# A new step list for block 0, other mask order, 54-key strided scores and a split last store

## The chip, the cores and the metric

One core of a Trainium2 chip runs the whole program once. The metric is device time in microseconds (us) of that core, the median of several runs. The engines have in-order queues of their own: TensorE (PE, with PEld for its weight loads), VectorE (DVE), ScalarE (ACT), GpSimd (POOL), and SyncE (SP), which here only issues DMAs. ACT issues a few DMAs too, from its own queue, between its activations.

## The reference

Eight batches of eight heads attend over 576 tokens (head width 64): four heads look back over 32 tokens, four over the tokens of the same remainder modulo 32. The attention output, 4608 tokens by 512, then goes through a gated layer of width 2048.

```python
scores = scale * np.matmul(q, k.transpose(0, 1, 3, 2))
mask_local = (rel >= 0) & (rel < stride)
mask_strided = (rel >= 0) & (pos[None, :] % stride == pos[:, None] % stride)
scores = np.where(masks[None, :, :, :], scores, -1000000000.0)
scores = scores - np.max(scores, axis=-1, keepdims=True)
attn = np.exp(scores)
attn = attn / (np.sum(attn, axis=-1, keepdims=True) + 1e-09)
return np.matmul(attn, v).astype(np.float32)
...
h = x @ w_in
g = h * (1.0 / (1.0 + np.exp(-h)))
return (g @ w_out).astype(np.float32)
```

## The kernel before

The layer runs in nine blocks of 512 tokens. A block has 16 chunks of 128 hidden columns; a chunk is 12 products of 128x512 for the hidden values (L623) and 12 for the output (L687), because each float32 operand is kept as a rounded high part and a low part and three of the four cross products are taken. Over the nine blocks this makes 3456 products, nearly all of PE's work.

Attention is cut into groups, six per batch: three local ones of 12 tiles of 32 queries, and three strided ones of 8, 8 and 6 tiles of 54 queries padded to 64. The first batch (groups 0 to 5) must be through before the first block can start, and in block 0 the weights are also split into their two parts. From block 1 on the groups of the next batches are worked between the chunks.

Everything up to the end of block 0 follows a list written out by hand, `PLAN` (L104): a word is a step, `~n` is n idle products of 128x128 on PE, and a letter behind a dot picks the engine. `follow` (L163) issues the steps in the order of the list, each on its own engine, and each engine works its steps in that order. For a group c: `k` and `v` load, `S` scores (PE, L402), `M` masking and row maximum (DVE, L422), `E` exponentials (ACT, L439, one per column of tiles and head), `R` reciprocal of the sum (DVE), `N` scaling (DVE or POOL, L458), `T` transposition (PE), `P` copy of it (DVE or ACT, L468), `O` product with v, `Q`, `X`, `B` the way back to x. `H0c` and `L0c` make the high and low part of x. For a piece i of weights: `p` load, `a` two activations (ACT, L266, L271), `j` (DVE, L277), `b` the high part (L318), `d` the low part (L322). For a chunk: `h` and `i` the two halves of the hidden products, `t`, `g`, `w`, `l` the gate and its two parts, `o` the output products. The first product, `h0`, needs `d0`, `L00` and `L01`.

Loads of k are split in block 0, and the second half of groups 0 to 2 is issued by ACT:

```python
ways = (load, nc.scalar.dma_start if a.at < 3 else load)
for some, way in zip(halved(n, 1 if a.b else 2), ways):
    way(out=kbds[kbd_of(a.b, a.at)][:, :, some], in_=kqt[a.b, a.gi, :, :, some])
```

POOL makes the masks at the start (L210 to L240): local ones of 64 keys, wide local ones of 96 keys (used from group 14 on), then the strided one, which group 3 is the first to use.

Of the kernel before, what the change touches and what calls it, by code (L numbers as in the profile page):

```python
# [13 lines left out]
F32 = mybir.dt.float32  # L14
# [10 lines left out]
DM, DFF = 512, 2048  # L25
STRIDE = 32
# [75 lines left out]
RATE = 310e3  # L102

PLAN = """  # L104
k0 k1 k2 k3 v0 ~9 S0 M0 k4 v1 E0 ~1 S1 k5 M1 E1 v2 ~1 S2 M2 E2 R0 ~2 T0 P0.D p0 S3 M3 E3 ~3 T1
P1.D R1 O0 Q0 S4 k6 M4 E4 v3 p1 T2 P2.D X0 B0.D O1 Q1 ~5 X1 R3 R2 S5 v4 B1.D v5 M5 E5 O2 N3.P
T3 p3 p5 H00.D R4 N4.P Q2 ~4 X2 P3.D L00.D R5 S6 B2.A H01.D N5.D a0 j0 L01.D T4 P4.A b0.D p2 a1
j1 d0.D O3 b1.D p4 k8 T5 P5.A O4 O5 d1.D p7 B3 p6 B4 H02.D L02.D B5 H03.A L03.D M6 a3 j3 b3.D
d3.D p9 a5 j5 a2 h0 h1 i0 t0 g0 i1 j2 t1 g1 h2 b5.A d5.D S8 k10 i2 w0.A l0.D h3 b2.A d2.D o0 v7
p11 a4 j4 b4.D d4.D w1.A l1.P M8 t2 g2 p8 a7 j7 b7.D S10 w2.D d7.D i3 p10 a9 j9 a6 j6 E8 R8  # L110
N8.D h4 b9.A o1 d9.P t3 g3 h5 M10 p13 E6 p15 v6 b6.D d6.D p12 k7 R6 l2.D o2 a10 j10 a11 j11
b11.D d11.D p17 h6 i4 a8 j8 i5 i6 a13 j13 b13.D w3.A l3.D N6.D V6 b8.A d8.P p14 o3 E10 t4 d13.P
p19 a15 j15 g4 O6 b10.A d10.P p16 t5 g5 h7 b15.D d15.D p21 a12 j12 v8 w4.A l4.D o4 a17 j17
b17.D d17.D p23 R10 i7 w5.A b12.A d12.D p18 a14 j14 a19 j19 B6 t6 g6 S7 k9 h8 l5.D o5 a16 j16
b16.D d16.D p22 V8 k12 M7 i8 t7 g7 O8 h9 v10 N10.P b19.A d19.P w6.A l6.P b14.A d14.D o6 p20 i9
a21 j21 a18 j18 b18.D a23 j23 b23.D w7.A l7.D o7 d23.D p25 a22 j22 b22.D d22.D p24 B8 E7 R7
N7.D t8 g8 h10 w8.A S9 l8.P k11 i10 V7 t9 g9 b21.A d21.P h11 d18.P o8 M9 a20 j20 a24 j24 b24.D
d24.D p26 t10 g10 h12 S11 k13 i12 b20.A d20.D i11 a25 j25 b25.D d25.D p27 E9 R9 V10 M11 w10.A
l10.P w9.A l9.P o9 t12 g12 t11 g11 N9.P a26 j26 b26.A d26.P p28 O7 B7 V9 v9 a27 j27 b27.D d27.D
O10 B10 E11 R11 N11.D o10 w11.A l11.P w12.A l12.P S12 M12 V11 a28 j28 b28.D d28.P E12 R12 N12.P  # L120
h13 h14 i13 t13 g13 i14 t14 g14 p29 a29 j29 b29.A d29.P O9 B9 v11 V12 o11 w13.A l13.P S13 M13
o12 w14.D l14.D p30 a30 j30 b30.D d30.D O11 B11 H10.A L10.D H11.A L11.D h15 H12.A H13.A L12.D
L13.D p31 a31 j31 b31.D d31.P o13 i15 t15 g15 w15.D l15.D E13 R13 N13.D V13 o14
"""


# [49 lines left out]
def sparse_attention_ffn(ctx: ExitStack, tc: tile.TileContext, kqt, vt, w_in, w_out, out):  # L176
# [31 lines left out]
    def mask(name, columns=72):  # L208
        m = const.tile([P, columns], F32, name=name)
        nc.gpsimd.memset(m, 0.0)  # L210
        return m
# [30 lines left out]
    nc.gpsimd.memset(ones, 0.0)
    for h in range(2):
# [43 lines left out]
    def halved(n, parts):  # L287
        return [slice(i * n // parts, (i + 1) * n // parts) for i in range(parts)]
# [62 lines left out]
    class Attention:  # L351


        def __init__(self, b, at):
            self.b, self.at, self.gi = b, at, order_of(b)[at]
            self.by_blocks = b * NG + at >= TURNED
            self.g = g = GROUPS[self.gi]
            self.spread = b * NG + at in SPREAD
            self.sums_by_pe = self.spread and g.local and not self.by_blocks
            self.kbd, self.vbd = kbds[kbd_of(b, at)], vbds[vbd_of(b, at)]  # L360
            self.cols = g.n * P
            self.wide = g.local and b * NG + at >= WIDE_FROM
# [15 lines left out]

        def halves(self, banks):

            n, keys = self.g.n, self.keys
            return [t[:, : n * keys].rearrange("p (c k) -> p c k", k=keys) for t in banks]

        def scores(self, banks=None):
            g, kbd = self.g, self.kbd
            self.pss = banks or [self.bank("pss") for _ in range(2)]
            if self.wide:
                for t in (0, 6, 2, 8, 4, 10):
                    c, r = self.at_of[t]
                    rows = slice(r * STRIDE, (r + 2) * STRIDE)  # L390
                    for h in range(2):
                        at = slice(h * D, (h + 1) * D)
                        nc.tensor.matmul(  # L393
                            self.pss[h][rows, c * WIDE : (c + 1) * WIDE],
                            kbd[at, 1, g.q0[t] : g.q0[t] + 2 * STRIDE],
                            kbd[at, 0, g.k0[t] : g.k0[t] + WIDE], start=True, stop=True,
                        )
                return
            for t, c, rows in self.tiles:
                for h in range(2):  # L400
                    at = slice(h * D, (h + 1) * D)
                    nc.tensor.matmul(  # L402
                        self.pss[h][rows, c * KW : (c + 1) * KW],
                        kbd[at, 1, g.q0[t] : g.q0[t] + g.rows],
                        kbd[at, 0, g.k0[t] : g.k0[t] + KW], start=True, stop=True,
                    )

        def peak(self):
            g = self.g
            s_ps = self.halves(self.pss)  # L410
            self.sm = att.tile([P, 640], F32, name="sm", bufs=3)
            self.s_sb = self.sm[:, : g.n * 2 * self.keys].rearrange(
                "p (c h k) -> p c h k", h=2, k=self.keys
            )
# [661 lines left out]
```

## Time and profile before

| | us |
|---|---|
| median of 3 runs (871.29 to 871.56) | 871.31 |
| the profiled execution | 871.88 |
| its span, first to last instruction | 870.1 |
| PE busy in the span | 862.5 |
| DVE, ACT, POOL busy | 514.1, 318.7, 40.3 |

The span is what the trace shows; 1.8 us of the profiled execution lie around it. A row of the timeline gives the start, the time to the end of the last one, engine, line, operation, tiles, shapes and how many equal ones were merged, and in brackets the idle time just before with the releaser. PE's ends are modelled and its products overlap, so starts are the better clock. In a table of stretches the columns are the stretch, its length, busy time and count of each engine, the granted PE clock as a share, the DMA engines' share and GB/s. A float32 product appears as two records.

### The profile page before, as it was taken

What the parts mean: (1) busy time and instruction counts of PE and PEld (TensorE: products, weight loads), DVE (VectorE), ACT (ScalarE), POOL (GpSimd) and SP (SyncE); (2) the same over time, 40 slices, a digit from 0 to 9 for tenths busy, and PEclk for the clock granted to TensorE, in tenths of its full rate; (3) what the DMA queues carried; (4) which work ended last, traced back from release to release, by engine and by line L of the source; (5) the groups of instructions that cost most, each with busy time, mean ns of one, the idle gap of its engine ahead of it and who ended that gap; (6) DMA issues with size and microseconds to landing.
All of it is one profiled execution on the core that took longest, in us unless ns stands there. A gap on an engine that the chain in (4) does not pass through costs nothing.

```text
span 870.1 us, 17241 instructions
## 1 busy us (share of the span) xinstructions
PE 862.5 (99%) x6809; PEld 707.9 (81%) x6809; DVE 514.1 (59%) x1602; ACT 318.7 (37%) x1070; POOL 40.3 (5%) x68
## 2 busy tenths in 40 slices
PE   8999999999999999999999999999999999999998
PEld 5777788888888888888888888888888888888886
DVE  6999887558556647656655855664762533343333
ACT  7987863315413333333431541333331311131111
POOL 5023320000000000000000000000000000000000
PEclk9999999999999999999999999999999999999999
DMA  9976443202302212220320230221210000000001
GB/s 293 288 251 221 142 157 95 72 2 76 118 1 72 77 50 68 72 77 18 100 73 1 77 117 1 72 76 50 69 29 1 29 20 1 1 27 22 1 1 49
DMA packets 37041, 64.55 MB, mean 74 GB/s; under 512 B 2912, under 2 KB 23776, under 8 KB 36960
## 3 DMA queue, kind: packets, MB, share of 16 engines
q1 hardware_dynamic: 36144, 62.79, 22.3%
q8 instruction: 53, 0.87, 0.4%
q10 hardware_dynamic: 816, 0.66, 0.2%
q14 instruction: 28, 0.23, 0.1%
HBM read 54.00 MB, written 9.44 MB: 73 GB/s over the span
## 4 chain that ended last, share of the span: by engine, by line
PE 92%; DVE 3%; ACT 2%; issue 1%; POOL 1%; POOLq 0%; DVEq 0%; ACTq 0%
PE po L687 44%; PE ps L623 43%; PE ps L526 3%; PE ps L393 1%; PE ps L402 1%; DVE stage L277 1%; DVE sm L422 1%; ACT stage L271 0%; ACT stage L266 0%; POOL mask_local L215 0%; DVE th L655 0%; DVE w L318 0%; ACT xb L566 0%; DVE w L322 0%; ACT sm L439 0%
## 5 line engine op out<-in xcount | busy, mean ns | idle before, releaser
L623 PE MATMUL ps<-xhi,w 128*128 128x512 f32 x1152 | 376.7, 390 | 0.5 <-DVE th L655 0.5
L623 PEld LDWEIGHTS ps<-xhi,w 128*128 128x128 f32 x1152 | 216.2, 188 | 46.0 <-DVE th L655 0.7
L655 DVE SCALAR_TENSOR_TENSOR th<-th,ps 128x512 f32<-128x512 f32 (+1 forms) x147 | 99.2, 675 | 258.6 <-ACT th L633 257.7
L633 ACT ACTIVATE th<-ps 128x512 f32<-128x512 f32 (+1 forms) x147 | 86.7, 590 | 448.3 <-PE ps L623 416.5
L623 PE MATMUL ps<-xlo,w 128*128 128x512 f32 x576 | 224.2, 389 | 0.0
L687 PE MATMUL po<-w,ghi 128*128 128x512 f32 x504 | 156.9, 392 | 0.0
L623 PEld LDWEIGHTS ps<-xlo,w 128*128 128x128 f32 x576 | 108.1, 188 | 22.2
L439 ACT ACTIVATE sm<-sm,sums 128x64 f32<-128x64 f32 (+1 forms) x320 | 109.2, 348 | 2.9 <-DVE sums L422 2.9
L687 PEld LDWEIGHTS po<-w,ghi 128*128 128x128 f32 x504 | 93.7, 188 | 20.0 <-DVE w L322 0.3
L667 DVE TENSOR_TENSOR glo<-th,ghi 128x512 fp32r<-128x512 f32 (+1 forms) x139 | 95.7, 689 | 11.9
L687 PE MATMUL po<-w,glo 128*128 128x512 f32 x252 | 98.4, 390 | 0.4 <-DVE glo L667 0.4
L687 PE MATMUL po<-stage,ghi 128*128 128x512 f32 x288 | 88.8, 389 | 0.0
L486 DVE STREAM_TRANSPOSE pt<-sm 32x192 f32<-32x192 f32 (+1 forms) x168 | 65.8, 392 | 3.0
L687 PE MATMUL po<-v,ghi 128*128 128x512 f32 x216 | 67.5, 394 | 0.0
L663 DVE CAST ghi<-th 128x512 fp32r<-128x512 f32 (+1 forms) x134 | 56.6, 422 | 12.8 <-PE po L687 1.2
L687 PEld LDWEIGHTS po<-stage,ghi 128*128 128x128 f32 x288 | 54.0, 188 | 11.2
L439 ACT ACTIVATION_READ_ACCUMULATOR sm<-sm,sums 128x1 f32 x320 | 61.8, 193 | 0.0
L687 PEld LDWEIGHTS po<-w,glo 128*128 128x128 f32 x252 | 47.3, 188 | 11.1 <-DVE glo L667 1.1
L687 PE MATMUL po<-stage,glo 128*128 128x512 f32 x144 | 56.0, 389 | 0.0
L687 PEld LDWEIGHTS po<-v,ghi 128*128 128x128 f32 x216 | 39.9, 188 | 8.4
L687 PE MATMUL po<-k,ghi 128*128 128x512 f32 x144 | 44.3, 389 | 0.0
L687 PE MATMUL po<-v,glo 128*128 128x512 f32 x108 | 42.0, 389 | 0.0
(77 smaller groups left out, 676.9 us busy)
## 6 DMA issues: line engine op xcount, KB each, us to landing
out<-stage SPq DMA_DIRECT2D x36, 256.0 KB, 2.0
v<-vt SPq DMA_DIRECT2D x21, 384.0 KB, 5.4
stage<-w_out SPq DMA_DIRECT2D x14, 512.0 KB, 4.3
k<-kqt SPq DMA_DIRECT2D x14, 512.0 KB, 4.9
stage<-w_in SPq DMA_DIRECT2D x12, 512.0 KB, 4.4
k<-kqt SPq DMA_DIRECT2D x14, 416.0 KB, 3.9
v<-vt SPq DMA_DIRECT2D x14, 256.0 KB, 5.4
k<-kqt SPq DMA_DIRECT2D x7, 448.0 KB, 3.9
```

The source lines that it names most:

```text
L277: nc.vector.scalar_tensor_tensor(out=upper, in0=upper, scalar=3, in1=lower, op0=ALU.logical_shift_left, op1=ALU.bitwise_or,)
L393: nc.tensor.matmul(self.pss[h][rows, c * WIDE : (c + 1) * WIDE], kbd[at, 1, g.q0[t] : g.q0[t] + 2 * STRIDE], kbd[at, 0, g.k0[t] : g.k0[t] ...
L402: nc.tensor.matmul(self.pss[h][rows, c * KW : (c + 1) * KW], kbd[at, 1, g.q0[t] : g.q0[t] + g.rows], kbd[at, 0, g.k0[t] : g.k0[t] + KW], s ...
L439: nc.scalar.activation(out=self.s_sb[:, c, h], in_=self.s_sb[:, c, h], func=AF.Exp, bias=self.peaks[:, c, h : h + 1], scale=-1.0, accum_ou ...
L486: nc.vector.transpose(out=pt[to, r % 2], in_=src[rows, 1 if self.wide else 1 - r % 2])
L526: nc.tensor.matmul(self.pso[p][h * D : (h + 1) * D, i * size : (i + 1) * size], vbd[at, 2 * i + h], moved, start=True, stop=True,)
L623: nc.tensor.matmul(ph, weight(0, wi, fc)[:, cc * P : (cc + 1) * P], x[xi][cc], start=(cc, n) == (0, 0), stop=(cc, n) == (NP - 1, 2),)
L633: nc.scalar.activation(out=th[:, cols], in_=ph[:, cols], func=AF.Tanh, scale=0.5)
L655: nc.vector.scalar_tensor_tensor(out=th[:, cols], in0=th[:, cols], scalar=1.0, in1=ph[:, cols], op0=ALU.add, op1=ALU.mult,)
L663: copy[engine](out=g[0][:, cols], in_=th[:, cols])
L667: either[engine].tensor_sub(out=g[1][:, cols], in0=th[:, cols], in1=g[0][:, cols].bitcast(F32))
L687: nc.tensor.matmul(po[tt], g[gi][:, cols], weight(1, wi, fc), start=fc == 0 and n == 0, stop=fc == NFC - 1 and n == 2,)
```

## The change

The list for block 0 is new. No subtraction `d` or `l` is on POOL until `d21`; in their place the two subtractions `L00` and `L01` are there. Steps change place throughout; the loads `k1`, `k2`, `k3` come behind `S0 M0 E0` and `S1`. The idle words sum to 21 instead of 25. POOL makes the wide masks behind the strided one. From group 14 on strided scores have 54 keys instead of 64, and POOL zeroes the ten columns left over in the tile `sm`. The very last store is cut into two halves, one scaled by DVE and stored by SP, one scaled and stored by ACT.

```diff
-k0 k1 k2 k3 v0 ~9 S0 M0 k4 v1 E0 ~1 S1 k5 M1 E1 v2 ~1 S2 M2 E2 R0 ~2 T0 P0.D p0 S3 M3 E3 ~3 T1
+k0 ~7 S0 M0 E0 k1 ~1 S1 k2 k3 v0 M1 E1 k4 R0 v1 ~3 S2 M2 E2 T0 P0.D R1 k5 v3 ~2 S3 M3 E3 T1
...
-    for wide, keys in ((False, KW), (True, WIDE)):
+    for wide, keys in ((False, KW),):
...
     masks[None, ()] = m
+    for wide, keys in ((True, WIDE),):
+        m = mask(f"mask_local{keys}", keys + 8)
...
+            self.seen = SEQ if not g.local and b * NG + at >= WIDE_FROM else self.keys
...
-                        self.pss[h][rows, c * KW : (c + 1) * KW],
+                        self.pss[h][rows, c * self.seen : (c + 1) * self.seen],
                         kbd[at, 1, g.q0[t] : g.q0[t] + g.rows],
-                        kbd[at, 0, g.k0[t] : g.k0[t] + KW], start=True, stop=True,
+                        kbd[at, 0, g.k0[t] : g.k0[t] + self.seen], start=True, stop=True,
...
+            if self.seen < self.keys:
+                pad = self.sm[:, : g.n * 2 * KW].rearrange("p (c k) -> p c k", k=KW)
+                nc.gpsimd.memset(pad[:, :, self.seen :], 0.0)
...
+            if (k, tt) == (NBLK - 1, NTT - 1):
+                r0 = k * T + tt * P
+                for some, engine in zip(halved(DM, 2), (nc.vector, nc.scalar)):
+                    if engine is nc.vector:
+                        nc.vector.tensor_scalar_mul(osb[:, some], po[tt][:, some], 0.5)
+                        nc.sync.dma_start(out=out[r0 : r0 + P, some], in_=osb[:, some])
+                    else:
+                        nc.scalar.mul(out=osb[:, some], in_=po[tt][:, some], mul=0.5)
+                        nc.scalar.dma_start(out=out[r0 : r0 + P, some], in_=osb[:, some])
+                continue
```

ACT at the start of the program, before: k_80 to k_82 are the tiles of groups 0 to 2, and an ACTIVATE at L439 (L457 in the changed file) is one of the exponentials `E`, six of them for a local group.

```order
L337 DMA k_80<-kqt 128x2x208
L337 DMA k_81<-kqt 128x2x224
L337 DMA k_82<-kqt 128x2x208
L439 ACT_TABLE_LOAD
L439 ACTIVATE sm,sums<-sm,sums 128x64 x40
L582 COPY xb<-po 128x3x4x32
```

ACT at the same place in the changed kernel:

```order
L351 DMA k_80<-kqt 128x2x208
L457 ACT_TABLE_LOAD
L457 ACTIVATE sm,sums<-sm,sums 128x64 x6
L351 DMA k_81<-kqt 128x2x224
L351 DMA k_82<-kqt 128x2x208
L457 ACTIVATE sm,sums<-sm,sums 128x64 x28
L617 CAST xhi<-xb 128x512
L457 ACTIVATE sm,sums<-sm,sums 128x64 x6
```

The second halves of k1 and k2 moved from ahead of all exponentials to behind the six of group 0, and `H00` moved in ahead of the last six.

POOL between the end of the masks and its third subtraction, before (xlo is the low part of x, glo of the gate, w of the weights, sm the scores):

```order
L242 MEMSET ones 128x2
L244 MEMSET ones 64x1 x2
L458 TENSOR_TENSOR sm<-sm,sums 128x512 x2
L667 TENSOR_TENSOR glo<-th,ghi 128x512
L322 TENSOR_TENSOR w_0_665<-stage_755,w_0_657 128x512
```

POOL at the same place in the changed kernel:

```order
L256 MEMSET ones 128x2
L258 MEMSET ones 64x1 x2
L476 TENSOR_TENSOR sm<-sm,sums 128x512
L621 TENSOR_TENSOR xlo<-xb,xhi 128x512 x2
L336 TENSOR_TENSOR w_0_696<-stage_1125,w_0_694 128x512
```

One scaling of scores left POOL, and the two low parts of x came to it, ahead of the first weights.

## Rows read from the trace of the kernel before

**Rows 1.** The page's first line, and three stretches from the table of stretches (columns as said above).

```profile
span 870.1 us, 17241 instructions
...
13.00:26.30 13.30, 12.06 (x315) 8.85 (x315) 12.89 (x60) 12.24 (x54) 2.09 (x2) 1.00 1.01 314
...
40.00:70.00 30.00, 29.11 (x234) 22.81 (x211) 29.36 (x64) 25.69 (x73) 7.67 (x6) 1.00 0.83 272
...
150.00:860.00 710.00, 710.00 (x5115) 588.51 (x5114) 381.45 (x1136) 203.10 (x701) 0.00 (x0) 1.00 0.14 45
```

**Rows 2.** Timeline of PE from its first idle products to `h0`: idle products, `S0`, `S1`, and the first product of `h0`.

```profile
1.37 4.21 PE L781 MATMUL ps<-ident 128*128 128x512 f32 x6 [1.37 <-POOL ident masks.py:199]
5.51 0.87 PE L402 MATMUL ps<-k 64*32 64x64 f32 x48
...
6.72 0.84 PE L402 MATMUL ps<-k 64*32 64x64 f32 x48
...
26.32 0.50 PE L623 MATMUL ps<-xhi,w 128*128 128x512 f32 x1
```

**Rows 3.** Timeline of ACT: its three DMA issues, the first exponential of `E0` and the first of `E1`.

```profile
0.74 2.23 ACTq L337 DMA_DIRECT2D k<-kqt  x3
...
6.86 0.35 ACT L439 ACTIVATE sm<-sm,sums 128x64 f32<-128x64 f32 x1 [2.58 <-DVE sums L422]
...
8.87 0.34 ACT L439 ACTIVATE sm<-sm,sums 128x64 f32<-128x64 f32 x1
```

**Rows 4.** DMA issues by line, with KB each and median us from issue to landing: the k loads issued by 1.0 us and by 2.5 us (ACT's), SP's loads of v issued from 7 to 11 us, and the stores of the whole run.

```profile
k<-kqt ACTq DMA_DIRECT2D x1, 208.0 KB, 4.0
...
k<-kqt ACTq DMA_DIRECT2D x1, 224.0 KB, 4.4
...
v<-vt SPq DMA_DIRECT2D x3, 192.0 KB, 4.3
...
out<-stage SPq DMA_DIRECT2D x36, 256.0 KB, 2.0
```

**Rows 5.** Timeline of DVE: the first instruction of `M0`, of `M1`, of `M3`, and `d0`.

```profile
6.59 0.23 DVE L422 CUSTOM_DVE_ANT_0 sm<-ps,mask 128x64 f32<-128x64 f32 x1 [6.59 <-PE ps L402]
...
7.71 0.23 DVE L422 CUSTOM_DVE_ANT_0 sm<-ps,mask 128x64 f32<-128x64 f32 x1 [0.17 <-POOL mask_local L215]
...
11.74 0.22 DVE L422 CUSTOM_DVE_ANT_0 sm<-ps,mask_strided 128x64 f32<-128x64 f32 x1 [1.08 <-POOL mask_strided L215]
...
24.89 0.69 DVE L322 TENSOR_TENSOR w<-stage,w 128x512 fp32r<-128x512 f32 x1
```

**Rows 6.** Groups of DVE instructions by form (busy us, mean ns of one, idle before them): `N` of a strided group of 8, `L`, `P` of 512 and of 384 columns; and from the timeline the start of `M6` and of the instruction behind it.

```profile
L458 DVE TENSOR_TENSOR sm<-sm,sums 128x512 f32<-128x512 f32 x13 | 9.0, 693 | 0.5
L603 DVE TENSOR_TENSOR xlo<-xb,xhi 128x512 fp32r<-128x512 f32 x8 | 5.5, 698 | 0.6 <-ACT xhi L599 0.6
L468 DVE COPY pt<-po 128x384 f32<-128x384 f32 x3 | 1.6, 541 | 0.0
L468 DVE COPY pt<-po 128x512 f32<-128x512 f32 x1 | 0.7, 679 | 0.0
28.61 0.22 DVE L422 CUSTOM_DVE_ANT_0 sm<-ps,mask 128x64 f32<-128x64 f32 x1
29.48 0.69 DVE L277 SCALAR_TENSOR_TENSOR stage<-stage 128x512 int32<-128x512 int32 x1
```

**Rows 7.** Timeline of POOL and DVE where they meet: a subtraction on POOL and the high part of a weight made by DVE inside it; the same DVE operation with POOL idle; another subtraction on POOL and DVE's transpositions inside it.

```profile
36.09 1.31 POOL L667 TENSOR_TENSOR glo<-th,ghi 128x512 fp32r<-128x512 f32 x1 [14.99 <-ACT ghi L663]
36.27 1.41 DVE L318 CAST w<-stage 128x512 fp32r<-128x512 f32 x1
...
30.20 0.43 DVE L318 CAST w<-stage 128x512 fp32r<-128x512 f32 x1
...
56.33 1.33 POOL L322 TENSOR_TENSOR w<-stage,w 128x512 fp32r<-128x512 f32 x1 [0.97 <-ACT w L318]
56.48 1.54 DVE L486 STREAM_TRANSPOSE pt<-sm 32x192 f32<-32x192 f32 x4
```

**Rows 8.** Timeline of PE in block 0: the rows before which it waited, each with the row ahead of it.

```profile
47.33 0.75 PE L687 MATMUL po<-w,ghi 128*128 128x512 f32 x2
48.46 0.50 PE L687 MATMUL po<-w,glo 128*128 128x512 f32 x1 [0.38 <-DVE glo L667]
...
66.15 0.69 PE L402 MATMUL ps<-k 64*64 64x64 f32 x32
67.36 0.50 PE L623 MATMUL ps<-xhi,w 128*128 128x512 f32 x1 [0.51 <-DVE th L655]
```

**Rows 9.** PE's strided scores in the timeline with the row behind them; and two groups by form, with 64 and with 54 columns moved.

```profile
83.77 0.69 PE L402 MATMUL ps<-k 64*64 64x64 f32 x32
84.39 0.50 PE L623 MATMUL ps<-xhi,w 128*128 128x512 f32 x1
...
L402 PE MATMUL ps<-k 64*64 64x64 f32 x704 | 15.5, 221 | 0.3 <-DVE sums L422 0.3
L526 PE MATMUL ps<-pt,v 64*64 64x54 f32 x616 | 13.2, 221 | 0.0
```

**Rows 10.** The end: one of the stretches in which the last four stores are written, and in the timeline ACT's scaling of the last output tile.

```profile
866.25:866.50 0.25, 0.07 (x1) 0.00 (x0) 0.18 (x1) 0.09 (x1) 0.00 (x0) 1.00 1.05 401
...
866.41 0.60 ACT L701 ACTIVATE stage<-po 128x512 f32<-128x512 f32 x1 [0.76 <-PE po L687]
```

More of the change, by code (lines that the diff above doesn't have):

```diff
@@ L104 @@
 PLAN = """
-k0 k1 k2 k3 v0 ~9 S0 M0 k4 v1 E0 ~1 S1 k5 M1 E1 v2 ~1 S2 M2 E2 R0 ~2 T0 P0.D p0 S3 M3 E3 ~3 T1
[L106 to L122, printed above, removed]
@@ L123 @@
-L13.D p31 a31 j31 b31.D d31.P o13 i15 t15 g15 w15.D l15.D E13 R13 N13.D V13 o14
+k0 ~7 S0 M0 E0 k1 ~1 S1 k2 k3 v0 M1 E1 k4 R0 v1 ~3 S2 M2 E2 T0 P0.D R1 k5 v3 ~2 S3 M3 E3 T1
+P1.D R2 v2 O0 Q0 p0 ~2 S4 k6 M4 X0 B0.D O1 Q1 R3 N3.P E4 T2 P2.D ~3 X1 B1.D H00.A S5 M5 O2 p1
+v4 T3 E5 R4 N4.D ~3 T4 v5 Q2 X2 B2.A p3 P3.D a0 P4.D L00.P R5 H01.D N5.D O3 B3 p5 p2 j0 L01.P
+S6 M6 k8 T5 P5.D a1 j1 b0.A d0 b1.D d1 p7 O4 B4 H02.A L02 p4 p6 O5 h0 h1 B5 H03.D L03 i0 i1 a3
+j3 b3.D a5 j5 d3 h2 p9 a2 j2 t0 g0 S8 k10 b5.A d5 p11 t1 g1 h3 w1.D b2.A d2 p8 i2 v6 w0.A l0 o0
@@ new lines @@
+l1 M8 i3 a7 j7 b7.D E6 R6 d7 p13 a4 j4 t2 g2 S10 k12 h4 N6 a9 j9 b4.A d4 o1 p10 a6 j6 M10 b9.A
+d9 p15 a11 j11 v7 i4 b6.A d6 p12 t3 g3 h5 V6 O6 v8 E8 R8 b11.A d11 p17 i5 a8 j8 N8 w2.A l2 o2
+a13 j13 a10 j10 b8.A d8 p14 t4 g4 h6 w3.A l3 o3 i6 b13.A d13 k7 a15 j15 b15.D d15 p21 b10.A d10
+p16 w4.A l4 o4 B6 t5 p19 a17 j17 b17.D d17 p23 g5 h7 S7 k9 i7 E10 R10 w5.D l5 a14 j14 t6 g6 h8
+a12 j12 b12.D d12 o5 p18 a21 j21 b21.D w6.A l6 a16 j16 i8 b14.A d14 p20 o6 a19 j19 a23 j23
+b16.A d16 p22 M7 V8 d21.P b23.A d23.P p25 t7 g7 w7.D l7 O8 v10 h9 o7 i9 b19.A d19 E7 R7 N7 a20
@@ new lines @@
+j20 B8 a22 j22 b22.D d22.D p24 t8 g8 h10 S9 i10 k11 a18 j18 a25 j25 b18.A d18 t9 g9 h11 M9 V7
+w8.A l8.P o8 b25.A d25.P p27 b20.A d20.P t10 g10 h12 S11 i12 a24 j24 b24.D d24.D p26 N10 V10
+M11 E9 w10.A l10.P i11 w9.A l9.P t12 o9 g12 t11 g11 O10 R9 N9 a27 j27 a26 j26 b26.D d26.D p28
+E11 R11 N11.P b27.A d27.P B10 O7 V9 B7 V11 v9 o10 w11.A l11.P w12.A l12.P S12 M12 a28 j28 b28.D
+d28.D E12 R12 N12.P h13 h14 i13 i14 t14 g14 t13 g13 O9 V12 B9 p29 a29 j29 b29.D d29.D o11 w13.A
+l13.P k13 S13 M13 p30 a30 j30 b30.D d30.D o12 w14.A l14.D v11 O11 B11 H10.A H11.A L11.D L10.D
@@ L124 @@
+h15 H12.A H13.A L13.D L12.D p31 a31 j31 b31.D d31.D o13 i15 t15 g15 w15.D l15.D E13 R13 N13.D
+V13 o14
 """
@@ L240, in sparse_attention_ffn @@
     masks[None, ()] = m
+    for wide, keys in ((True, WIDE),):
+        m = mask(f"mask_local{keys}", keys + 8)
+        for t in range(P // STRIDE):
+            ahead = STRIDE * (t % 2) if wide else 0
+            keep(m, t * STRIDE, STRIDE, [keys], [1], -1 - ahead, -1)
+            keep(m, t * STRIDE, STRIDE, [keys], [-1], STRIDE + ahead, 1)
+        masks[wide, ()] = m
+        some = {s for g in GROUPS for s in (g.paired_starts if wide else g.starts) if s}
+        for starts in sorted(some):
+            first = const.tile([P, keys + 8], F32, name=f"mask{keys}_" + "".join(map(str, starts)))
+            nc.gpsimd.tensor_copy(out=first, in_=m)
+            for t in starts:
+                keep(first, t * STRIDE, STRIDE, [keys], [1], -STRIDE, 0)
+            masks[wide, starts] = first
     ones = const.tile([P, 2], F32, name="ones")
@@ L379, in halves @@
         def halves(self, banks):
-            n, keys = self.g.n, self.keys
+            n, keys = self.g.n, self.seen
             return [t[:, : n * keys].rearrange("p (c k) -> p c k", k=keys) for t in banks]
@@ L413, in peak @@
                 "p (c h k) -> p c h k", h=2, k=self.keys
-            )
+            )[:, :, :, : self.seen]
+            if self.seen < self.keys:
+                pad = self.sm[:, : g.n * 2 * KW].rearrange("p (c k) -> p c k", k=KW)
+                nc.gpsimd.memset(pad[:, :, self.seen :], 0.0)
             s_sb = self.s_sb
@@ L417, in peak @@
             self.peaks, self.rsum = peaks, rsum = sums[:, 0, : g.n], sums[:, 1, : g.n]
-            self.inv = rsum.unsqueeze(3).broadcast_to([P, g.n, 2, self.keys])
+            self.inv = rsum.unsqueeze(3).broadcast_to([P, g.n, 2, self.seen])
             for c in range(g.n):
@@ L422, in peak @@
                     nc.vector.tensor_tensor_reduce(
-                        out=s_sb[:, c, h], in0=s_ps[h][:, c], in1=self.masks[c][:, : self.keys],
+                        out=s_sb[:, c, h], in0=s_ps[h][:, c], in1=self.masks[c][:, : self.seen],
                         scale=-SCALE, scalar=BIG, op0=ALU.add, op1=ALU.min,
@@ L428, in lessen @@
         def lessen(self):
-            peaks = self.peaks.unsqueeze(3).broadcast_to([P, self.g.n, 2, self.keys])
+            peaks = self.peaks.unsqueeze(3).broadcast_to([P, self.g.n, 2, self.seen])
             nc.gpsimd.tensor_sub(self.s_sb, self.s_sb, peaks)
```

## The prediction

> **What bounds the kernel now.** I read the table of stretches first, then the timelines of PE, ACT and DVE in the first 30 us, the DMA issues, and last the few waits of PE. From 150 to 860 us PE is busy throughout, and DVE, ACT and the DMA engines are far from full [rows 1]. Products start in a fixed pace there, so nothing that DVE or ACT do in the later blocks can show. What can change is the time before the first product `h0`, at 26.32 us [rows 2], the waits of PE in block 0, and the end. In the head ACT and DVE are nearly full (12.24 and 12.89 of 13.30 us), and in block 0 DVE is (29.36 of 30) [rows 1]. The chain of the head runs: k0 lands, `S0`, `M0`, `E0`, then the exponentials of all groups one after the other on ACT, with DVE between, until `d0` at 24.89 to 25.58 [rows 5]; PE comes to `h0` 0.74 later.
>
> **The loads on ACT's queue.** This is the term on which I rest. Before, ACT issues its three halves of k0, k1 and k2 from 0.74 on and then waits for `M0` [rows 3]. In the new order the halves of k1 and k2 stand behind the six exponentials of `E0` on the same in-order queue, and `E0` waits for `M0`, `S0` and k0. Behind them in turn wait `S1`, `M1`, `E1`, and SP, whose load of k5 writes the tile that `S1` reads.
>
> When do they go out? Nine idle units before `S0` take 5.51 - 1.37 = 4.14 us, 0.46 each [rows 2]; seven take 3.2, to 4.6. k0 was issued at 0.74 and takes 4.0 to land [rows 3, 4], so `S0` starts at 4.8 instead of 5.51, and `E0` at 6.15 instead of 6.86. Six exponentials take 8.87 - 6.86 = 2.01 [rows 3]; the issue comes at 8.1. For the landing the rows give 2.0 (a lone store, late in the run) up to 4.4 (the load of k1 itself, with the start's traffic) and 4.3 (v, 7 to 11 us) [rows 4]. SP has fewer loads in flight here than in those, since it stops at k5, but more than none: I take 3.2, so the half is there at 11.3. Two of the twelve tiles of `S1` need only the first half; the other ten and the step to DVE take about 0.9 of the 7.71 - 6.72 = 0.99 that `S1` to `M1` took [rows 2, 5]. `M1` starts at 12.2 instead of 7.71: +4.5 us. Bounds: 11.0 and 13.4.
>
> **From `M1` to `d0` on DVE.** Before, this took 25.58 - 7.71 = 17.87 us. The new list puts in ahead of `d0`: two copies `P` that were ACT's (0.68 and 0.54), `M6` (29.48 - 28.61 = 0.87) and one scaling `N` (0.69); it takes out `L00` and `L01` (0.70 each), a high part of a weight and one of x (0.43 each, by the weight's row) [rows 6, 7]. Sum: 2.78 - 2.26 = +0.5. The wait of 1.08 for the strided mask [rows 5] goes: POOL makes it right after the narrow ones. Three idle units instead of one stand between `S1` and `S2`, so `M2` is late by some 0.9 (two units of 0.46). And there are the two subtractions that POOL gets.
>
> DVE suffers from those by what it does at the time. A high part of a weight takes 1.41 inside a subtraction on POOL and 0.43 without, 1.0 more; four transpositions take 1.54 either way [rows 7]. `L00` starts when `H00` is done, about when DVE comes to its scaling `N4`; `L01` starts behind `H01`, just ahead of `j0`. Each can cost DVE 0 to 1.0. The Trainium skill has a rule for this (SBUF — State Buffer, section "Who interferes with whom"): a VectorE instruction with two SBUF inputs contends with a GpSimd instruction that reads SBUF, and whichever issues first holds the shared ports while the other blocks. `N4` reads the scores and sums, `j0` two halves of a weight, so by that rule both meet it and the cost is up to 2.0; the row of 1.41 agrees with full blocking. From the rows alone I take 0.7 for the two, bounds 0 and 2.0.
>
> Together 17.9 + 0.5 - 1.1 + 0.9 + 0.7 = 18.9, so `d0` ends at 31.1 and `h0` starts there, since PE, with 21 idle units instead of 25 and all of its work behind the same chain, is not later: **h0 moves from 26.3 to 31.1, +4.8 us**. From here to the end PE only has its fixed work and its waits, so this goes into the time in full.
>
> **Waits of PE in block 0.** Three are seen: 48.46 - 47.33 = 1.13 where two starts are 0.46 apart otherwise, so 0.65; 67.36 - 66.15 = 1.21 against 84.39 - 83.77 = 0.62, so 0.6 [rows 8, 9]; and some smaller, which I put at 0.25. In all 1.5. The new list takes six POOL subtractions out of the stretch in which they hit DVE, at 1.0 lost each against the 0.6 to 0.7 that the same work costs on DVE, and puts more hidden products ahead of the second output product. Against that it gives DVE the ones that lay beside transpositions and cost it nothing [rows 7]. DVE is full there, so I let two thirds of the waits go: **-1.0 us**, bounds -1.5 and +1.0.
>
> **54 keys.** 32 records take 0.62 [rows 9]. If they went by columns, ten of 64 less would give 0.1 us for a group, and 17 groups have it: -1.6 at most. But 64 and 54 columns have the same 221 ns a record [rows 9], the four parts of the array work side by side, and weights must be loaded for each; I take **0**, and +0.5 for the other end (a start delay of some 30 ns a group). DVE's and ACT's saving and POOL's 17 small fillings lie under PE's work, and would cost only if a mask step came late by whole chunks. **The wide masks** are needed from group 14 on, after block 0: nothing.
>
> **The last store.** Scaling 256 instead of 512 columns on each of two engines would save part of the 0.60 of the last scaling [rows 10]. But the DMA engines are already full, 1.05 of their capacity, with the three stores before it: the megabyte of the four stores sets the end, and halving rows does not make it smaller. I take **+0.1** for twice as many, shorter packets; bounds -0.3 and +0.3.
>
> **Sum.** +4.8 - 1.0 + 0 + 0.1 = +3.9. On the profiled execution's 871.88 (span 870.1 and 1.8 around it) that is 875.8; it lay 0.57 above the median of the runs, so on the median 871.31 the forecast is **875.2 us**.
>
> **Rivals.**
> A. *The late issue does not matter*, because the half is not held behind `E0` or lands while ACT is still busy. For it: `S2` and `E2` have slack of their own. Against it: ACT's rows are strictly in the order of its program, and its queue issued all three before it did anything else [rows 3]. Then `E1` follows `E0` at 8.1 instead of 8.87, the head is 0.7 shorter, less 0 to 1.0 for the collisions: -0.7 - 1.0 + 0.1 = -1.6, 869.7, at least partly beyond 0.2%: this is the faster side. The Trainium skill (DMA: Bandwidth & Descriptors, section "Issuing engines are not separate DMA queues") says that starting DMAs from several engines only saves the sequencer's time of issue, usually small beside the transfer; by that, which queue holds the half would not matter, and 869.7 would be the time. No run here has yet shown a load behind a waiting activation. Chance 0.09, of it 0.07 faster and 0.02 same.
> B. *Held, but caught up*: it lands in 2.0 (`M1` at 11.0, +3.3), no collision (-0.7), the waits all go (-1.5) and the products gain half of their bound (-0.4). Then 871.31 + 4.8 - 1.2 - 0.7 - 1.5 - 0.4 = 872.3, same. It needs all of them; 0.07.
> C. *Held, and DVE falls behind for good*: the half lands in 4.4 (+1.2), both collisions in full (+1.3), and in block 0 DVE's extra work makes PE wait 1.0 more than before instead of less (+2.0): 875.2 + 4.5 = 879.7; half of it, 877.5, is likelier. It decides once DVE's list from `h0` to the second output product is later than PE's. For it: 29.36 busy of 30. Slower too; 0.15.
>
> **Chances.** The forecast has 0.69, C 0.15, B 0.07, A 0.09. Faster or slower counts from 0.2%, 1.74 us, about what a measurement can tell here. Faster: A's 0.07, and 0.01 from the forecast's if A and B come together. Same: B's 0.07, A's 0.02, and 0.03 from the forecast's own lower edge, 0.12. Slower: the rest, 0.80. The range leaves out A, about half of B and C's upper half, 0.2 in all: 872.2 to 878.0.
>
> **What would show it.** ACT's two DMA issues behind six exponentials at about 8 us; `M1` at about 12.2, with DVE and ACT idle for 3 to 4 us before it; no mask wait at `M3`; `h0` at 31.1; a DVE instruction of 1.4 us or more beside `L00` or `L01`; fewer waits of PE between 45 and 70 us; 32 records of 54 keys in the same 0.62; the last stores ending as long after the last product as before. I am wrong if `M1` starts before 9 us, if `h0` is before 28, or if the waits in block 0 grow beyond 2.5 us.

## The result and the profile after

The changed kernel takes **878.21 us** (median of 4 runs, 877.77 to 878.85) against 871.31 (871.29 to 871.56): the ratio is 1.0079 with a 95% interval of 1.0066 to 1.0091, so it is slower by 0.8%, 6.9 us. The forecast was 875.2 with a range of 872.2 to 878.0. The sign and the late issue of two loads are as forecast; the size is too small, and the time lies 0.2 us above the range. The profiled execution took 877.77.

The table of stretches of the changed kernel, its first line and the stretches of the head and of block 0 (columns as in [rows 1]):

```profile
span 876.0 us, 17274 instructions
...
4.00:6.50 2.50, 2.50 (x60) 1.47 (x58) 0.72 (x9) 0.45 (x3) 2.00 (x10) 1.00 1.08 352
6.50:12.80 6.30, 0.21 (x8) 0.04 (x5) 0.24 (x4) 1.65 (x10) 4.44 (x20) 0.75 0.85 276
12.80:15.00 2.20, 2.19 (x42) 1.16 (x42) 1.12 (x14) 0.89 (x5) 0.00 (x0) 0.50 0.08 24
15.00:20.00 5.00, 4.76 (x143) 3.22 (x143) 3.73 (x36) 4.73 (x29) 0.00 (x0) 0.85 0.82 236
...
40.00:70.00 30.00, 30.00 (x266) 24.15 (x265) 29.45 (x80) 29.94 (x82) 0.00 (x0) 1.00 0.94 314
```

From 6.5 to 12.8 us PE, DVE and ACT work 0.21, 0.24 and 1.65 us, and the DMA engines stand at 0.85 of their capacity: the core waits for a load. In block 0, 40 to 70 us, PE is busy for all of the 30 us; before it was 29.11 [rows 1]. The timeline of PE says which load (answers to [rows 2]):

```profile
4.64 0.97 PE L417 MATMUL ps<-k 64*32 64x64 f32 x48
...
6.27 0.44 PE L417 MATMUL ps<-k 64*32 64x64 f32 x8
12.81 0.90 PE L417 MATMUL ps<-k 64*32 64x64 f32 x40 [6.11 <-DMA k<-kqt]
...
33.89 0.50 PE L641 MATMUL ps<-xhi,w 128*128 128x512 f32 x1
```

`S1` does the 8 records that need only the first half of k1, then PE waits 6.11 us for the second. `h0` is at 33.89 instead of 26.32. The timeline of ACT shows the late issues (answers to [rows 3]); of the exponentials the first, the last three and the first of `E1` are shown:

```profile
0.73 0.67 ACTq L351 DMA_DIRECT2D k<-kqt  x1
...
6.05 0.35 ACT L457 ACTIVATE sm<-sm,sums 128x64 f32<-128x64 f32 x1 [3.34 <-DVE sums L440]
...
6.78 0.55 ACTq L351 DMA_DIRECT2D k<-kqt  x1
...
7.06 0.33 ACT L457 ACTIVATE sm<-sm,sums 128x64 f32<-128x64 f32 x1
...
7.37 0.62 ACTq L351 DMA_DIRECT2D k<-kqt  x1
7.39 0.33 ACT L457 ACTIVATE sm<-sm,sums 128x64 f32<-128x64 f32 x1
...
7.72 0.33 ACT L457 ACTIVATE sm<-sm,sums 128x64 f32<-128x64 f32 x1
...
14.11 0.35 ACT L457 ACTIVATE sm<-sm,sums 128x64 f32<-128x64 f32 x1 [5.97 <-DVE sums L440]
```

What SP had sent by then, and how long the half took, stand in its timeline and in the DMA issues around 6.78 us (answers to [rows 4]):

```profile
0.73 3.27 SPq L351 DMA_DIRECT2D k<-kqt  x5
4.04 1.07 SPq L356 DMA_DIRECT2D v<-vt  x2
5.58 1.20 SPq L351 DMA_DIRECT2D k<-kqt  x2
6.82 1.32 SPq L356 DMA_DIRECT2D v<-vt  x2
13.59 1.20 SPq L351 DMA_DIRECT2D k<-kqt  x2
```

```profile
k<-kqt ACTq DMA_DIRECT2D x1, 224.0 KB, 6.0
```

SP issues k3, v0 and k4 ahead of 6.78 and v1 right behind, and stops only at k5, which it issues at 13.59, about when `S1` is through. The half takes 6.0 us and lands at 12.8. Last, DVE and POOL where the subtractions `L00` and `L01` run on POOL (answers to [rows 7]), and the only wait of PE behind `h0` that the timeline shows:

```profile
13.85 0.23 DVE L440 CUSTOM_DVE_ANT_0 sm<-ps,mask 128x64 f32<-128x64 f32 x1 [7.11 <-PE ps L417]
...
24.97 1.19 DVE L472 TENSOR_SCALAR sums<-sums 128x8 f32<-128x8 f32 x1
...
29.98 1.65 DVE L291 SCALAR_TENSOR_TENSOR stage<-stage 128x512 int32<-128x512 int32 x1
...
24.87 1.27 POOL L621 TENSOR_TENSOR xlo<-xb,xhi 128x512 fp32r<-128x512 f32 x1 [0.40 <-ACT xhi L617]
29.54 1.53 POOL L621 TENSOR_TENSOR xlo<-xb,xhi 128x512 fp32r<-128x512 f32 x1 [3.40 <-DVE xhi L617]
...
121.95 0.47 PE L641 MATMUL ps<-xhi,w 128*128 128x512 f32 x1 [0.63 <-DVE sums L440]
```

`M1` starts at 13.85 instead of 7.71 [rows 5]. The first step of `R4`, on 8 columns, takes 1.19 beside `L00`, and `j0` takes 1.65 beside `L01`.

### The profile page after: what moved, and what is told of

The parts are those of the page before. It is cut to its first block, busy times and chain, and to the rows that moved or that the text cites. A ratio compares the mean times of both kernels' runs of the same rounds, so it can differ in the third digit from the quotient of the medians.

```text
span 876.0 us, 17274 instructions
## 1 busy us (share of the span) xinstructions
PE 861.1 (98%) x6805; PEld 706.9 (81%) x6805; DVE 514.0 (59%) x1607; ACT 319.2 (36%) x1074; POOL 32.0 (4%) x77
## 4 chain that ended last, share of the span: by engine, by line
PE 96%; DMA 1%; DVE 1%; ACT 1%; SPq 0%; issue 0%; POOL 0%; POOLq 0%; ACTq 0%; DVEq 0%
PE ps L641 45%; PE po L705 45%; PE ps L544 3%; PE ps L417 2%; PE ps L408 1%; PE ps L809 1%; DMA k<-kqt 1%; DMA stage<-w_in 0%; DVE stage L291 0%; SPq L356 0%; SPq L323 0%; DVE sm L440 0%; ACT xb L584 0%; DVE th L673 0%; DVE pt L504 0%
## 5 line engine op out<-in xcount | busy, mean ns | idle before, releaser
L457 ACT ACTIVATE sm<-sm,sums 128x54 f32<-128x54 f32 (+2 forms) x320 | 108.1, 343 | 9.9 <-DVE sums L440 9.9
L457 ACT ACTIVATION_READ_ACCUMULATOR sm<-sm,sums 128x1 f32 x320 | 61.0, 191 | 0.0
```

Of the source, the lines that this page charges most:

```text
L457: nc.scalar.activation(out=self.s_sb[:, c, h], in_=self.s_sb[:, c, h], func=AF.Exp, bias=self.peaks[:, c, h : h + 1], scale=-1.0, accum_ou ...
```

## The experiments

Each kernel ran with the kernel before on the same chip; on the three chips that one had a median of 871.38, 871.30 and 871.42. The starts are those of the profiled execution of each, read from the timelines; "rest" is from `h0` to the start of the last product. Where `M1` comes before ACT is about to end `E0` (8.87 us in the kernel before, 7.8 to 8.1 with the new list), `E1` still waits for ACT, so "M1 to h0" holds up to 0.9 of slack there (1.16 from `M1` to `E1` in [rows 3, 5], 0.26 in the changed kernel).

| kernel | M1 | h0 | M1 to h0 | rest | median | ratio to before, interval |
|---|---|---|---|---|---|---|
| before | 7.71 | 26.32 | 18.61 | 839.61 | 871.31 | |
| changed | 13.85 | 33.89 | 20.04 | 837.96 | 878.21 | 1.0079 (1.0066, 1.0091) |
| halves first on ACT | 7.00 | 27.08 | 20.08 | 838.01 | 871.01 | 0.9992 (0.9983, 1.0000) |
| halves on SP | 7.25 | 27.02 | 19.77 | 837.98 | 870.95 | 1.0000 (0.9992, 1.0009) |
| L00, L01 on DVE | 13.63 | 33.14 | 19.51 | 837.97 | 877.55 | 1.0068 (1.0056, 1.0080) |
| fewer loads ahead | 10.84 | 31.58 | 20.74 | 837.99 | 875.52 | 1.0047 (1.0035, 1.0059) |
| 14 idle products | 12.99 | 34.27 | 21.28 | 837.99 | 877.84 | 1.0068 (1.0055, 1.0081) |
| 28 idle products | 14.03 | 33.25 | 19.22 | 838.09 | 876.76 | 1.0058 (1.0042, 1.0073) |
| halves first, L00, L01 on DVE | 7.50 | 26.93 | 19.43 | 837.96 | 870.34 | 0.9987 (0.9979, 0.9996) |
| halves first, L00, L01 on DVE, M6 later | 8.16 | 26.38 | 18.22 | 838.86 | 870.43 | 0.9986 (0.9977, 0.9995) |
| halves first, L00, L01 on DVE, old keys and store | 7.86 | 26.95 | 19.09 | 838.15 | 870.53 | 0.9991 (0.9982, 1.0001) |
| before, late halves | 14.94 | 34.09 | 19.15 | 839.58 | 878.76 | 1.0082 (1.0068, 1.0096) |
| before, new mask order | 8.32 | 25.30 | 16.98 | 839.57 | 871.02 | 0.9995 (0.9986, 1.0004) |

**The halves first on ACT.** The order on all engines but ACT stays the changed one.

```diff
-k0 ~7 S0 M0 E0 k1 ~1 S1 k2 k3 v0 M1 E1 k4
+k0 ~7 S0 M0 k1 k2 E0 ~1 S1 k3 v0 M1 E1 k4
```

> The changed kernel with one thing undone: the second halves of k1 and k2 are again issued by ACT ahead of the exponentials of E0; the order on every other engine, SP's loads too, is the changed one. Theory 1 (the place of these two DMAs on ACT's queue holds up the whole head): M1 starts at about 7.2 us instead of 13.85, h0 at 26.3 to 27.3 instead of 33.9, the time is 870.5 to 872.0, about 6.8 us under the changed kernel. Rival (the new list is itself slower up to h0, by its two subtractions on POOL and by what it puts on DVE, and the late load only uses up slack): h0 not under 30, time 875 or more.

`M1` starts at 7.00, `h0` at 27.08, the time is 871.01: two DMAs on one queue carry all of the loss, and the rest of the change, taken together, makes no difference that the times can tell. In the traces it works both ways: `h0` is 0.76 later than in the kernel before, and what follows is 1.60 shorter. The timeline of ACT in this run:

```profile
0.73 1.96 ACTq L351 DMA_DIRECT2D k<-kqt  x3
2.72 1.28 ACT L457 ACT_TABLE_LOAD   x1 [2.72 <-issue]
5.77 0.35 ACT L457 ACTIVATE sm<-sm,sums 128x64 f32<-128x64 f32 x1 [1.76 <-DVE sums L440]
```

**The halves on SP.**

```diff
-        ways = (load, nc.scalar.dma_start if a.at < 3 else load)
+        ways = (load, nc.scalar.dma_start if a.at < 1 else load)
```

> The changed kernel with the second halves of k1 and k2 issued by SP, in the place that the list gives them; ACT issues that of k0 alone. Theory 1 (what is late is the issue, held by ACT's wait for M0): SP issues the half of k1 at about 2.1 us, it lands by 6 us, M1 starts at 7.0 to 7.5, the time is within 1 us of the run in which ACT issues it first (870.5 to 872.5). Rival (two queues bring the halves in faster than one, and the split itself is what counts): M1 after 9 us, time 873.5 or more.

`M1` at 7.25 and 870.95 us: as theory 1 has it, though the single runs spread wider than before, from 870.27 to 874.08. Which of the two queues sends the halves makes no difference to the median; what stands ahead of them on it does.

**The kernel before with late halves.** The changed order of ACT's first instructions alone, in the old list:

```diff
-k0 k1 k2 k3 v0 ~9 S0 M0 k4 v1 E0 ~1 S1 k5
+k0 ~9 S0 M0 E0 k1 k2 k3 v0 k4 v1 ~1 S1 k5
```

> The kernel before with one move alone: k1, k2, k3, v0, k4 and v1 behind E0 in the list, so that on SP nothing changes and on ACT the halves of k1 and k2 stand behind the exponentials of group 0. Theory 1: ACT issues the half of k1 at 7.2 to 7.6 us, behind what SP has issued by then it lands at 12.5 to 13.5, M1 starts at 13.5 to 14.5 instead of 7.71, and the time is 877 to 879, as much as the whole change costs. Rival (the old list has the slack to catch up, and the new list is needed for the loss): under 874.

878.76: the old list with this one move loses 7.5 us. The issue is at 7.64 and the flight 6.2 us, so the half lands at 13.9 and `M1` starts at 14.94, both 0.4 later than I had allowed. In the timeline of ACT, and in the DMA issues at 7.6 us:

```profile
6.91 0.35 ACT L439 ACTIVATE sm<-sm,sums 128x64 f32<-128x64 f32 x1 [4.20 <-DVE sums L422]
...
7.64 0.55 ACTq L337 DMA_DIRECT2D k<-kqt  x1
...
15.21 0.35 ACT L439 ACTIVATE sm<-sm,sums 128x64 f32<-128x64 f32 x1 [6.20 <-DVE sums L422]
```

```profile
k<-kqt ACTq DMA_DIRECT2D x1, 224.0 KB, 6.2
```

**Fewer loads ahead of the late half.** The issue stays late, but SP meets k5, and with it its wait, before k4 and v1:

```diff
-v0 M1 E1 k4 R0 v1 ~3 S2 M2 E2 T0 P0.D R1 k5 v3
+v0 M1 E1 R0 ~3 S2 M2 E2 T0 P0.D R1 k5 k4 v1 v3
```

> The changed kernel with the loads k4 and v1 put behind k5 in the list, so that SP, which waits at k5 for S1, has four loads fewer on their way when ACT issues the late half of k1; its issue stays at about 6.8 us. Theory 2 (the DMA engines work off their loads in order of issue and are full, so a late issue also has to wait for all that SP issued meanwhile): the half lands at 9.5 to 10.5 instead of 12.8, M1 starts at 10.5 to 11.5, and the time is 875.0 to 876.5. Rival (a load from ACT's queue takes its 6 us here whatever SP has issued): it lands at 12.8 again, the time is 878.2 or a little more.

The timeline of SP, and the DMA issue at 6.58 us:

```profile
0.73 3.27 SPq L351 DMA_DIRECT2D k<-kqt  x5
4.04 1.07 SPq L356 DMA_DIRECT2D v<-vt  x2
10.59 2.52 SPq L351 DMA_DIRECT2D k<-kqt  x4
```

```profile
k<-kqt ACTq DMA_DIRECT2D x1, 224.0 KB, 3.2
```

Without the four loads the half takes 3.2 instead of 6.0 us, `M1` is at 10.84, and the time falls by 2.7 to 875.52: the flight depends on what SP has sent, not on the queue that the half is on. This is as theory 2 has it; that the engines work strictly in the order of issue is not shown by it. `M1` comes 3.0 earlier and the time falls by less, since `M1` to `h0` grew by 0.7: ACT waits 0.46 for DVE ahead of `E3` here, with a granted clock of 0.50 from 12.8 to 15 us, and k4 and v1 go out only behind k5, which SP issues at 10.59. Which of the two it is was not tried.

**L00 and L01 on DVE.**

```diff
-L00.P R5 H01.D N5.D O3 B3 p5 p2 j0 L01.P
+L00 R5 H01.D N5.D O3 B3 p5 p2 j0 L01
```

> The changed kernel with the two subtractions L00 and L01 on DVE instead of POOL, the late loads kept. Theory (each made one DVE instruction wait in full, 1.02 and 0.96 us, on the path to h0): DVE loses these 1.98 and gains two subtractions of 0.69, so h0 is 0.6 earlier, at 33.3, and the time 877.6; no DVE instruction beside them takes over 0.7. Rival (the waits lay in DVE's slack): h0 is later by up to 1.4, the time 878.8 to 879.6.

877.55 and `h0` at 33.14, as the theory has it; 0.22 of the 0.75 by which `h0` is earlier is an earlier `M1`. The times alone would not show it: the runs go from 877.04 to 878.39, those of the changed kernel from 877.77 to 878.85. The two instructions of DVE, now with POOL idle:

```profile
25.13 0.17 DVE L472 TENSOR_SCALAR sums<-sums 128x8 f32<-128x8 f32 x1
...
29.58 0.68 DVE L291 SCALAR_TENSOR_TENSOR stage<-stage 128x512 int32<-128x512 int32 x1
```

0.17 and 0.68 instead of 1.19 and 1.65: the collisions cost DVE 1.99 us, the two subtractions there 1.38.

**Both together.** The halves first on ACT, and `L00` and `L01` on DVE, each by the diff above.

> The changed kernel with both: ACT issues the halves of k1 and k2 first, and L00 and L01 are on DVE. In the run with the halves first, M1 starts at 7.0, ACT is full to the end of E5, and h0 comes at 27.08. Theory (the two waits of DVE, 1.0 each, lie on the path there too): h0 at 26.4, the time 870.3 (870.0 to 870.6), under the kernel before by 1.0. Rival (with the loads in time another chain, over ACT, ends last): no gain, 871.0.

870.34, as expected, and faster than the kernel before by 0.13% beyond its interval. That it is faster than the halves first alone (871.01) the intervals do not tell, and the trace shows less than the theory: `h0` at 26.93 is 0.5 later than expected and 0.15 earlier than with the halves first alone. `M1` was 0.5 later in this execution, but `E1` only 0.18, since it waits for `E0`; from `E1` to `h0` it took 0.33 less, where 0.7 was expected.

**PE kept busy.** Idle products ahead of `S1`, 14 and in a later run 28:

```diff
-k0 ~7 S0 M0 E0 k1 ~1 S1 k2 k3
+k0 ~7 S0 M0 E0 k1 ~14 S1 k2 k3
```

> The changed kernel with fourteen idle products instead of one ahead of S1, so that PE works until shortly before the late half of k1 lands instead of standing still for 6.1 us. Theory 3 (PE's granted clock, 0.75 from 6.5 to 12.8 us and 0.50 from 12.8 to 15, is a small price of its own that comes with the wait): the clock stays at 1.00, M1 starts at 13.7 to 13.9 as before, M2 1.7 us behind it instead of 2.36, ACT's wait of 0.27 ahead of E2 goes, and the time is 877.5 to 877.9. Rival (the clock is what makes the head late): 2 us or more are gained, 876 or less. Rival (the products lie in time that nobody waits for): 878.2.

> The changed kernel with 28 idle products ahead of S1. The run with 14 did not tell the clock's price, since they took 3.1 us and PE stood still for 3 us behind them; 28 take 6.3 us, from 5.5 to 11.9. Theory 3: the granted clock is 1.00 from 12.8 to 15 us, M1 to M2 takes 1.7 us as in the run with the halves first, but M3 to M4 takes the 0.7 back that it had lost less, since ACT is then full, so M1 to h0 stays at 20.0 and the time at 877.6 to 878.5. Rival (the slow clock is a price): M1 to h0 19.3 and the time 877.4 or less.

Stretches from 6.5 to 20 us, with 14:

```profile
6.50:12.80 6.30, 3.13 (x55) 1.59 (x53) 0.00 (x0) 1.37 (x9) 4.44 (x20) 0.89 0.90 312
12.80:15.00 2.20, 2.20 (x44) 1.12 (x44) 1.23 (x14) 1.74 (x11) 0.00 (x0) 0.50 0.34 95
15.00:20.00 5.00, 5.00 (x121) 3.48 (x103) 3.23 (x32) 3.72 (x23) 0.00 (x0) 0.68 0.81 247
```

And with 28, with the first exponential of `E1` behind them:

```profile
6.50:12.80 6.30, 6.18 (x22) 2.57 (x20) 0.23 (x4) 1.64 (x10) 4.44 (x20) 1.00 0.85 284
12.80:15.00 2.20, 1.76 (x70) 1.12 (x77) 0.97 (x13) 0.70 (x5) 0.00 (x0) 1.00 0.03 10
15.00:20.00 5.00, 4.67 (x169) 3.45 (x151) 4.47 (x39) 5.00 (x32) 0.00 (x0) 1.00 0.85 230
...
14.29 0.35 ACT L457 ACTIVATE sm<-sm,sums 128x64 f32<-128x64 f32 x1 [6.15 <-DVE sums L440]
```

Fourteen failed as a test: they filled only half of the wait, PE stood still for 3.17 us, and the granted clock was 0.50 (1.2 GHz) from 12.8 to 15 us all the same, and 0.68 up to 20. Its time lies in the range of theory 3, but for another reason: the half landed earlier in that execution (`M1` at 12.99), and `M1` to `h0` took 21.28. With 28 the clock stays at 1.00 (2.4 GHz), and `M1` to `h0` falls from 20.04 to 19.22. So the rival is right and my theory 3 wrong: the slow clock costs time on the path to `h0`, 0.8 us by these two executions. Counted from the first exponential of `E1`, which takes the slack out, `h0` follows after 33.89 - 14.11 = 19.78 us in the changed kernel, after 18.96 with 28 idle products, and after 19.31 and 18.98 with the halves first on ACT and on SP, whose clock was 1.00 throughout; so the price is 0.5 to 0.8. With 14, whose clock stayed low for longer, it is 21.01. The median fell by 1.45, to 876.76; how much of the rest is the chip or the landing of the half was not tried.

**The new mask order in the kernel before.** The masks are made in the order of the changed kernel, the list stays.

> The kernel before with the wide masks made behind the strided one and nothing else. My prediction took DVE's wait of 1.08 us ahead of M3 off the path to h0. Theory of the prediction: the time falls by about 1.1 to 870.2. Rival (ACT's exponentials run without a gap from 6.86 us on, E2's last is at 12.5, and M3 at 11.74 is early enough for E3): h0 stays at 26.3 and the time at 871.1 to 871.5.

Neither clearly. In the profiled executions `h0` is 1.02 earlier, as the prediction's step has it, though `M1` is later, at 8.32, and DVE goes into `M3` at 11.05 without a wait; but the median falls by 0.28 alone, which the interval does not tell from nothing. The lowest run is 870.36, against 871.25 for the lowest of the kernel before.

**M6 later**, on top of both together:

```diff
-S6 M6 k8 T5 P5.D a1 j1 b0.A d0 b1.D d1 p7
+S6 k8 T5 P5.D a1 j1 b0.A d0 b1.D d1 M6 p7
```

> The run with the halves first and L00 and L01 on DVE, and in addition M6 (0.87 us of DVE, 24.57 to 25.44 there) moved in the list from ahead of T5 to behind d1. Theory (after E5 the path to h0 is DVE's list: M6 stands ahead of P5, P5 of O5, O5 of h0): P5 at 24.6, h0 0.7 to 0.9 earlier at the same M1, the time 869.5 (869.2 to 870.0), faster than the kernel before beyond its interval. Rival (ACT's copies or d0 take its place at once): h0 not moved, 870.3.

`h0` is 0.55 earlier behind an `M1` that is 0.66 later, as the theory has it, but the rest grows by 0.90, and the time does not move: the rival's time, by another place than it named. In the timeline of PE behind `h0`:

```profile
34.95 0.50 PE L641 MATMUL ps<-xhi,w 128*128 128x512 f32 x1 [0.49 <-DVE th L673]
```

The work of DVE that left the head is now ahead of the gate `t` of the first chunks, which PE waits for; this wait is 0.49 of the 0.90.

**Old keys and store**, on top of both together, with `self.seen = self.keys` for all groups and without the branch of the last store:

> The run with the halves first and L00 and L01 on DVE, with 64 keys in all strided scores and the last store in one piece, as in the kernel before. By the traces of before and after a chunk that takes in 24 or 32 strided records has a gap of 2.488 and 2.605 us with 64 keys, 2.480 and 2.597 with 54; the last product is 4.16 us from the end with one store, 4.13 with two. Theory: the gaps read 2.488 and 2.605 again, the 17 groups make 0.13 us, the end 4.1 to 4.2, and the time 870.3 to 870.6, not to be told from the run with both edits. Rival (POOL's 17 fillings or the new store cost or bring more): over 0.5 away.

As expected: 870.53, which is not to be told from 870.34. The gaps between two products with strided records between them read 2.488 and 2.605 with 64 keys and 2.480 and 2.597 with 54, 8 ns a group, 0.13 us for 17. From the start of the last product to the end of the span it is 4.2 us with one store and 4.1 with two, as far as the one decimal of the spans tells.

## Why the prediction was right in sign and short in size

**The late issue: right.** ACT's two DMAs went out behind `E0`'s wait, and `S1`, `M1`, `E1` and SP's k5 stood behind them. Putting these two back takes away 7.2 us of a loss of 6.9, and moving them alone in the old list loses 7.5. Rival A, by which the late issue would not matter, is out. What it drew from the Trainium skill (DMA: Bandwidth & Descriptors, section "Issuing engines are not separate DMA queues"), that starting DMAs from several engines saves only the sequencer's time of issue, agrees with the runs in which no wait stands ahead of the halves: 870.95 us from SP, 871.01 from ACT. That sentence does not speak of a wait ahead of the DMA on its queue, and this is what cost the time here.

**The landing: the step that failed.** The prediction took 3.2 us from issue to landing, with bounds of 2.0 and 4.4, because "SP has fewer loads in flight here than in those, since it stops at k5". It does stop there, but k4 and v1 stand ahead of k5 in the new list, and nothing holds SP up before. With these in the way the half took 6.0, and without them 3.2. The issue itself was 1.3 earlier than taken (6.78 for 8.1): it came 0.05 after the last instruction of `M0`, for which `E0` waits (6.51 to 6.73), and not behind the work of `E0`. So `M1`: 6.78 + 6.0 + 1.07 = 13.85 against the forecast's 8.1 + 3.2 + 0.9 = 12.2, 1.65 too low and above the bound of 13.4.

**From M1 to h0:** 18.9 was forecast, 20.04 measured. Two terms were short. The collisions were taken at 0.7 of a possible 2.0; they cost 1.99. The Trainium skill (SBUF — State Buffer, section "Who interferes with whom"), by which the second to issue blocks in full, agrees with this: the 8-column step of `R4` came 0.10 us behind `L00` and took 1.19. It was this step and not `N4`, behind it, that met `L00`. And the clock was no term at all, though a late `S1`, and so a stop of PE, was forecast: 0.5 to 0.8. Together that is 1.8 to 2.1, and 1.14 was missing, so the rest of the working came 0.7 to 1.0 too high. [Rows 3, 5] hold the reason, which was overlooked: `M1` at 7.71 had slack, since `E1` came at 8.87 only, when ACT was through with `E0`. In the changed kernel `E1` follows `M1` by 0.26, so 0.9 of the 6.14 by which `M1` is late costs nothing. That the mask wait's 1.08 lay on the path to `h0` is borne out by the trace of its own run (1.02), though not by the median. The last link of the path was another than forecast, with little effect on the sum. DVE's rows of `d0`, and of PE ahead of `h0`:

```profile
33.48 0.68 DVE L336 TENSOR_TENSOR w<-stage,w 128x512 fp32r<-128x512 f32 x1
...
33.06 0.91 PE L529 MATMUL po<-pt,v 64*64 64x54 f32 x24 [1.39 <-ACT xb L584]
33.89 0.50 PE L641 MATMUL ps<-xhi,w 128*128 128x512 f32 x1
```

The first product of `h0` starts at 33.89, before `d0` ends at 34.16. It follows `O5`, which had waited 1.39 us; only later products of `h0` read the low part that `d0` makes.

**Waits of PE in block 0: right, and somewhat more.** -1.0 was forecast, two thirds of 1.5. In 40 to 70 us they are all gone, one new wait of 0.63 stands at 121.95, and the rest is 839.61 - 837.96 = 1.65 shorter, 0.13 of it by the keys. So the waits that went come to about 1.65 - 0.13 + 0.63 = 2.15, more than the 1.5 that the prediction saw. Each run with the new list has about this rest, but for the one with M6 moved. Rival C, which let these waits grow, is wrong there; its late landing and its full collisions came about.

**54 keys** bring 0.13, taken at 0 (bounds -1.6 and +0.5). **The last store** changes nothing, taken at +0.1: from 872 to 874.5 us the DMA engines stand at 1.01 to 1.09 of their capacity, and the end waits for them as before. Nor do the two halves run side by side: ACT's scaling starts only when DVE's is done, as the row behind the stretch shows.

```profile
872.50:873.00 0.50, 0.00 (x0) 0.00 (x0) 0.20 (x1) 0.21 (x1) 0.00 (x0) 1.00 1.05 402
...
872.78 0.38 ACT L722 ACTIVATE stage<-po 128x256 f32<-128x256 f32 x1 [1.22 <-DVE stage L719]
```

**The sum.** `h0` +7.57, the rest -1.65, the end (4.17 us from the last product's start before, 4.15 after) -0.02: +5.9, which is the spans' 876.0 - 870.1. Forecast was +3.9. The other 1.0 up to the medians' 6.9 is where the profiled executions lie: that of before 0.57 above its median, that of the changed kernel 0.44 below. The forecast took the first of these into account (it counts from the median), but could not know the second. So 2.0 of the 3.0 that it fell short lie in the working (1.65 up to `M1` and 1.14 from there to `h0`, less 0.65 and 0.12 for what follows), and 1.0 in where the profiled executions lie.

## What to carry to other kernels

A DMA on the queue of an engine that also computes was issued here only when the waits ahead of it were over (at 6.78 us), and its flight then depended on the loads that another queue had sent meanwhile (6.0 us, and 3.2 with four fewer): its price is the wait and the backlog, and the backlog has to be read from the list of loads up to the first one that truly blocks. So a load that starts a chain goes ahead of the first waiting instruction, or to a queue without work of its own. And when a wait makes PE stand still, the slower clock behind it (0.50 here, at a price of 0.5 to 0.8 us) is a term of the sum as well.

## What was not expected of the hardware

- ACT's DMA at 7.37 went out while the last two exponentials ahead of it in the program had not started (7.39 and 7.72): the issue was held by the waits of the instructions ahead, not by their work. With 14 idle products this DMA went out only at 8.31, when all six were through; why was not looked into.
- Behind a stop of PE of 3.17 us (14 idle products) the granted clock was 0.50, as it was behind one of 6.11 us.
- With the same issues in the same order, the second half of k1 landed 3.7 us after its issue in one execution (halves first on ACT) and 5.4 in another (M6 later). The kernel before seems to hide this: 35 of its 65 runs beside the experiments lie within 871.25 to 871.4, though the highest is 873.03, while the one without the mask wait at `M3` runs from 870.36 to 872.26. That the wait pins the head at a fixed time, so that an early landing does not show, would explain it; it was argued from these spreads and not tried further.
